# A sigmoid-attention and swish-MLP kernel on one core: its opening joins the step table, and the table is laid out anew

## The chip, the core and the metric

The kernel runs on one core of a Trainium2 chip. A core has a matrix engine (PE, or TensorE, whose weight loads the profile lists as PEld), a vector engine (DVE), a scalar engine (ACT), a general engine (POOL, or GpSimd) and a queue engine that only starts transfers here (SP). Each runs its own list of instructions in order and waits on semaphores for the others. Operands lie in SBUF, an on-chip memory of 128 partitions; PE writes its results to PSUM, eight banks of 128 x 512 float32. Transfers between main memory and SBUF (DMA) are issued by SP and POOL and carried out by 16 shared DMA engines.

The metric is the device time of one execution in microseconds (us). Three runs of the kernel before took 368.27, 368.7 and 368.22 us; their median is 368.27.

## The reference

```python
scores = q @ k.T / sqrt(64) - log(448)             # 8 batches, 12 heads, 448 tokens, 64 values a head
attn   = 1 / (1 + exp(-scores))                    # a sigmoid, no softmax
x      = (attn @ v).transpose(0, 2, 1, 3).reshape(3584, 768)
h      = x @ w_in                                  # 768 x 2048
g      = h / (1 + exp(-beta * h))                  # beta: one value for each of the 2048
out    = g @ w_out                                 # 2048 x 768
```

Everything comes and goes as float32; the kernel computes in float16 with float32 sums.

## The kernel before

The work on PE is of three kinds. *Score visits* multiply 32 rows at a time, four or more small products side by side in the array (line 221); ACT turns each PSUM tile of scores into float16 weights by a sigmoid (line 233). *Value blocks* multiply these with v in halves of 64 columns (line 294, `attend`); DVE copies the result, rounded to float16, to `xT` (line 303). *Dense steps* are the two layers of the MLP (line 174, `dense`), on the full 128 x 128 array, or cut into two halves of 64 columns where `tiled["cols"]` is 64. Most of the dense work uses Strassen-Winograd products: seven products of half-size blocks replace eight, at the price of sums of blocks on DVE.

The program is one flat order of steps, written in a table of tokens (`STEPS`) that `follow` runs one by one. A token is a letter and its numbers. `V g.jt` is a score visit for four heads (group g; three groups make a batch) and one block of keys; `A g` the value block of that group. `D b.dc` is one plain dense step of the first layer (batch b, columns dc): six matmuls, a sigmoid on ACT and a product on DVE that frees its bank. `O` is the plain second layer of the first tokens. `I b.d.i` is the i-th Winograd product of the first layer, six matmuls of 224 columns each; `I...1` is followed by an ACT copy to an output buffer, `I...2` by two ACT sigmoids, the others by DVE sums. `U t.i.part` is the same for the second layer and output tiles t and t+1: four matmuls of 384 columns each; the second part of `U...3` stores tile t, that of `U...4` tile t+1. `G` and `B` are a sigmoid on ACT and a product on POOL that reads an output buffer. `X` and `H` are token and hidden sums on DVE, `S` and `T` sums of weights on DVE (1536 elements each), `R` transposes q (`.0`) or k (`.1`) on DVE, `E` doubles a part of v. `Q g` loads q and k of a group and `K b` the v of a batch; both are issued by POOL, in POOL's order with its products. Output tiles are stored by SP, four transfers a tile.

Four buffers (`outp`, 4 x [128, 896] float32) hold both the output tiles and the intermediate results of `I`; they rotate, so a store has to land before its buffer is written again. Three buffers hold raw q and k. PSUM is shared out as two score tiles of two banks and four single banks after the opening (three score tiles and two banks before; `share_psum`). `bank` always takes the single bank that has been unused longest, so a step can wait for the copy or product that frees it. In `follow` a dense step is cut into halves if the next visit or value block is an `A`.

The opening, up to the first tokens, is no part of the table. It is written as Python: all its loads first, then transposes, six half visits (224 of 448 queries) with filler matmuls (`idle_units`, whose result nobody reads) behind each, then value blocks, further half visits and the first half (columns 0 to 223) of the plain first layer, 16 steps by `first_half`:

```python
        for n in range(2 * QPB):
            half_visit(n // 2, 0, n % 2)
            idle_units((3, 4, 4, 4, 2, 2)[n])
        double_v_last(0)
        transpose(0, 0, NH, NB)
        attend(0, 0, QH)
```

Of the kernel before, what the change touches and what calls it, by code (L numbers as in the profile page):

```python
# [13 lines left out]
def kernel(  # L14
# [267 lines left out]
    def attend(g: int, c0: int, n: int, part=(0, 1)):  # L282
# [4 lines left out]
        avs = [bank("av_ps") for _ in slots]  # L287
        order = sorted(range(JF), key=lambda jt: list(at_tiles).index((slots[-1], jt, c0)))
        todo = [(s, av, jt) for jt in order for s, av in zip(slots, avs)]
        for s, av, jt in todo + [(s, av, JF) for s, av in zip(slots, avs)]:  # L290
            at = at_tiles.pop((s, jt, c0))
            base, nk = (last_base(s), KL) if jt == JF else (0, P)
            for hh in range(2):
                nc.tensor.matmul(  # L294
                    av[hh * D : (hh + 1) * D, 0:n],
                    vs[b][base : base + nk, 2 * (s % NPAIR) + hh, jt],
                    at[base : base + nk, hh, 0:n],
                    start=(jt == order[0]),
                    stop=(jt == JF),
                    tile_position=(base, hh * D),  # L300
                )
        for s, av in zip(slots, avs):
            nc.vector.tensor_copy(out=xTs[b][:, s % NPAIR, c0 : c0 + n], in_=av[:, 0:n])  # L303
# [304 lines left out]
    todo = list(range(NDC))  # L608

    def first_half(n: int):  # L610
        for _ in range(n):
            dense1(0, todo.pop(0), 0, QH)
# [28 lines left out]
    def follow(steps):  # L641
        last_visit = max(i for i, step in enumerate(steps) if step[0] == "V")
        nearer = [""] * len(steps)
        for i in reversed(range(len(steps) - 1)):
# [9 lines left out]
        R3.1 R3.0 D0.6 D0.12 R4.1 D0.14 D0.7 V3.1 R4.0 D0.13 D0.0 D0.8 V3.0 D0.3 D0.9 V3.3 D0.1  # L654
        D0.10 E1 D0.2 Q6 V3.2 D0.4 O0.0.0 D0.5 O0.0.1 O0.0.2 V4.1 O1.0.0 O0.0.3 A3 V4.0 O1.0.1 R5.1
        D0.11 D0.15 O0.0.4 R5.0 V4.2 O0.0.5 S1.1 O0.0.6 O1.0.2 O1.0.3 S1.0 O0.0.7 S2.0 O1.0.4 V4.3
        O1.0.5 A4 V5.1 O1.0.6 O0.1.0 O0.1.1 O1.1.0 S2.1 Q7 T3.1 O1.0.7 S4.0 T2.1 O0.1.2 V5.0 T3.0
        O0.1.3 O1.1.1 K2 O1.1.2 O1.1.3 O0.1.4 O0.1.5 V5.2 T2.0 O1.1.4 O0.1.6 O0.1.7 R6.1 O1.1.5 R6.0
# [6 lines left out]
        I2.0.2 H4.1 I2.0.3 R10.1 X2.2 U4.1.0 V9.0 X2.3 U4.1.1 Q11 G2.0 U4.6.0 U4.6.1 Q12 A9 V10.0
        I2.0.7 H4.3 U4.5.0 U4.7.0 U4.5.1 V10.1 U4.7.1 I2.0.4 B2.0.1 U4.3.0 U4.4.0 U4.2.0 B2.0.0
        U4.2.1 R11.0 U4.3.1 U4.4.1 R11.1 I2.1.1 V10.2 Q13 Q14 I2.1.6 I2.1.5 I2.1.7 I2.1.2 K4 I2.1.3
        V10.3 I2.1.4 G2.1 B2.1.0 R12.1 I2.2.1 B2.1.1 A10 V11.0 I2.2.6 I2.2.5 R12.0 I2.2.7 I2.2.2
        I2.2.3 I2.3.1 Q15 G2.2 V11.1 I2.3.6 I2.2.4 B2.2.1 B2.2.0 I2.3.5 I2.3.2 R13.1 I2.3.7 I2.3.3
        V11.2 I2.3.4 B2.3.1 U6.1.0 B2.3.0 H6.2 U6.1.1 A11 H6.0 V12.2 U6.2.0 U6.7.0 H6.1 U6.2.1 G2.3  # L670
# [6 lines left out]
        B3.2.1 I3.3.2 I3.3.7 I3.3.3 V14.3 I3.3.4 U10.1.0 B3.3.0 B3.3.1 H10.2 R16.0 U10.1.1 A14 V15.2
        U10.2.0 H10.0 U10.7.0 H10.1 G3.3 U10.2.1 U10.5.0 U10.6.0 U10.6.1 H10.3 U10.5.1 X4.0 V15.0
        U10.7.1 X4.1 U10.3.0 U10.3.1 I4.0.1 I4.0.6 I4.0.5 H12.0 U10.4.0 X4.2 U10.4.1 X4.3 I4.0.2
        I4.0.3 I4.0.7 V15.1 E5 K6 G4.0 Q19 H12.2 U12.1.0 H12.1 U12.1.1 A15 R17.0 V16.1 U12.2.0 R18.1  # L680
        I4.0.4 B4.0.0 U12.6.0 B4.0.1 U12.2.1 U12.5.0 V16.2 U12.6.1 U12.5.1 I4.1.1 H12.3 I4.1.6
        U12.7.0 U12.7.1 R17.1 I4.1.5 U12.3.0 U12.3.1 I4.1.2 V16.0 R18.0 I4.1.3 U12.4.0 I4.1.7
        U12.4.1 Q20 G4.1 V16.3 I4.1.4 A16 B4.1.0 B4.1.1 R19.0 V17.2 I4.2.1 I4.3.1 I4.2.6 I4.2.5
        V17.1 I4.2.2 Q21 I4.2.7 I4.2.3 G4.2 V17.0 I4.2.4 I4.3.6 B4.2.0 I4.3.5 I4.3.7 I4.3.2 B4.2.1
        R20.0 I4.3.3 G4.3 V18.2 I4.3.4 R19.1 A17 I5.0.1 B4.3.0 X5.0 B4.3.1 U14.1.0 V18.0 I5.0.2 X5.1
        I5.0.6 Q22 I5.0.5 U14.1.1 V18.1 X5.2 X5.3 H14.0 I5.0.3 U14.2.0 E6 H14.2 K7 I5.0.7 H14.1
        V18.3 G5.0 U14.2.1 A18 V19.2 I5.0.4 U14.6.0 U14.5.0 U14.7.0 B5.0.0 U14.6.1 U14.5.1 B5.0.1
        U14.7.1 I5.1.1 V19.0 H14.3 I5.1.6 I5.1.2 U14.3.0 R21.1 U14.3.1 R20.1 V19.1 U14.4.0 E7 I5.1.5
        I5.1.7 U14.4.1 I5.1.3 V20.0 R21.0 I5.1.4 G5.1 B5.1.0 I5.2.1 B5.1.1 A19 V20.2 I5.2.6 Q23
        I5.2.5 I5.2.2 I5.2.7 I5.2.3 I5.3.1 I5.2.4 G5.2 I5.3.6 B5.2.0 V20.3 I5.3.5 I5.3.7 B5.2.1  # L690
        I5.3.2 I5.3.3 I5.3.4 V20.1 X6.0 B5.3.1 H16.2 B5.3.0 U16.1.0 U16.1.1 A20 V21.2 U16.2.0 H16.0
        U16.7.0 U16.2.1 G5.3 V21.0 H16.1 U16.5.0 R23.1 U16.6.0 U16.6.1 H16.3 U16.5.1 U16.7.1 H18.2
        I6.0.1 X6.2 V21.1 U16.3.0 X6.1 U16.3.1 U16.4.0 U16.4.1 I6.0.6 R22.1 I6.0.2 R22.0 I6.0.5 A21
        V22.0 H18.0 X6.3 I6.0.3 H18.1 U18.1.0 U18.7.0 U18.1.1 V22.1 I6.0.7 U18.6.0 U18.6.1 V22.2
        I6.0.4 H18.3 U18.5.0 G6.0 U18.2.0 R23.0 U18.5.1 U18.2.1 B6.0.1 B6.0.0 U18.7.1 V22.3 U18.3.0
        U18.3.1 U18.4.0 U18.4.1 I6.1.1 I6.1.6 A22 V23.0 I6.1.5 I6.1.7 I6.1.2 I6.1.3 I6.2.1 G6.1
        I6.1.4 B6.1.0 I6.2.6 I6.2.5 B6.1.1 I6.2.2 V23.1 I6.2.7 I6.2.3 I6.3.1 I6.2.4 I6.3.6 G6.2
        B6.2.1 I6.3.5 B6.2.0 I6.3.7 I6.3.2 I6.3.3 V23.2 I6.3.4 B6.3.1 U20.1.0 H20.2 U20.1.1 A23
        U20.7.0 B6.3.0 U22.1.0 H20.0 U20.2.0 H20.1 X7.0 U20.2.1 U20.5.0 U20.6.0 G6.3 U20.6.1 I7.0.1
        U20.5.1 H20.3 X7.2 U22.1.1 U20.7.1 I7.0.2 X7.1 U20.3.0 U20.3.1 U22.2.0 U22.2.1 H22.0 U20.4.0  # L700
        X7.3 H22.2 H22.1 U20.4.1 U22.5.0 I7.0.6 I7.0.5 U22.7.0 I7.0.7 I7.0.3 U22.6.0 G7.0 I7.0.4
        I7.1.1 I7.1.6 I7.1.5 B7.0.0 B7.0.1 I7.1.2 I7.1.7 I7.2.1 I7.1.3 I7.2.6 G7.1 I7.1.4 I7.2.5
        I7.2.7 B7.1.0 B7.1.1 U22.6.1 I7.2.2 I7.2.3 U22.5.1 H22.3 I7.2.4 I7.3.1 I7.3.6 B7.2.0 I7.3.5
        G7.2 B7.2.1 I7.3.7 U22.7.1 I7.3.2 I7.3.3 U24.1.0 I7.3.4 U22.3.0 U22.3.1 U24.1.1 U22.4.0
        B7.3.0 U22.4.1 U24.2.0 B7.3.1 H24.0 U26.1.0 U24.2.1 H24.1 U24.5.0 G7.3 U24.6.0 H24.2 U24.6.1
        U24.5.1 H24.3 H26.0 U24.7.0 U24.7.1 U26.1.1 U24.3.0 U24.3.1 H26.1 U24.4.0 U26.2.1 U26.5.0
# [159 lines left out]
```

## Time and profile before

| | |
|---|---|
| median of three runs | 368.27 us |
| span of the profiled execution | 367.6 us |
| PE, DVE, ACT, POOL busy | 361.6, 272.2, 248.7, 154.3 us |
| PE waits that the profile names, 150 ns or longer | 2.3 us in five places |
| loads issued by POOL, moved | 22.47 MB |
| stores and first loads issued by SP, moved | 11.71 MB |
| granted PE clock | 0.9 or more in each of the 40 slices |

The span goes from the first instruction of the program to the last. A group's row reads: source line, engine, operation, output and inputs by name, shapes, count, then busy time in us, mean ns of one, and the idle time of the engine before these instructions with what ended it. A row of a stretch gives its length, then the busy time of PE, PEld, DVE, ACT and POOL with the number of instructions, the granted clock, and two figures on DMA. A row of the timeline gives start, length, engine and instructions that follow each other; lengths overlap, since a matmul's end is modelled and the next one starts before it, so a step's cost is read from start to start. The chain of waits is followed back from the last instruction to whatever released it.

### The profile page before, as it was taken

Reading aid. Unit: us, or ns where it says so; the run is one execution under the profiler, and the core shown is the slowest. Engines: PE = TensorE matmul, PEld = TensorE weight load, DVE = VectorE, ACT = ScalarE, POOL = GpSimd, SP = SyncE. Lnnn points to the kernel's source line nnn. Section 1 sums busy time; section 2 is a strip of 40 time slices with the busy share of each in tenths; the row PEclk is TensorE's granted clock in tenths of the full one; section 3 lists DMA queues with packets and bytes.
Section 4 is the critical chain, followed back from the end, with each engine's and each line's share of the span. In section 5 each row is a group of like instructions: output and inputs, shape, how many; then the busy total and the mean of one; then the engine's idle time right before and its main releaser. Section 6 shows DMA issues by size and latency. Waiting matters only on the chain.

```text
span 367.6 us, 9130 instructions
## 1 busy us (share of the span) xinstructions
PE 361.6 (98%) x3677; PEld 237.7 (65%) x3677; DVE 272.2 (74%) x524; ACT 248.7 (68%) x410; POOL 154.3 (42%) x192
## 2 busy tenths in 40 slices
...
GB/s 163 182 197 201 197 206 199 237 40 2 50 139 52 165 147 2 81 57 122 143 9 153 52 137 51 50 79 88 52 1 88 2 87 2 0 87 0 61 67 134
DMA packets 42698, 34.76 MB, mean 95 GB/s; under 512 B 21904, under 2 KB 39200, under 8 KB 42656
## 3 DMA queue, kind: packets, MB, share of 16 engines
q0 software_dynamic: 36688, 22.47, 44.7%
q1 hardware_dynamic: 5968, 11.71, 11.5%
...
q14 instruction: 13, 0.11, 0.1%
...
## 4 chain that ended last, share of the span: by engine, by line
PE 94%; DMA 3%; ACT 1%; DVE 1%; SPq 0%; issue 0%; ACTq 0%; DVEq 0%
PE m_ps L174 71%; PE sco L221 12%; PE av_ps L294 10%; DMA out_dram<-osb 2%; PE idle_ps L743 1%; ACT attnT L233 1%; DMA gt<-in_k_dram 1%; DVE osb L375 0%; SPq L605 0%; ACT osb L428 0%; DVE xT L303 0%; ACT osb L466 0%; DVE raw L760 0%; SPq L726 0%; DVE kT L763 0%
## 5 line engine op out<-in xcount | busy, mean ns | idle before, releaser
L233 ACT ACTIVATE attnT<-sco 128x896 f16<-128x896 f32 (+1 forms) x163 | 139.2, 908 | 38.5 <-PE sco L221 37.9
L375 DVE TENSOR_TENSOR osb<-m_ps,osb 128x448 f32<-128x448 f32 (+2 forms) x197 | 116.3, 596 | 51.7 <-PE m_ps L174 42.2
L174 PEld LDWEIGHTS <-w_in 128*128 128x128 f16 (+1 forms) x948 | 81.0, 100 | 19.4 <-issue 11.5
L174 PE MATMUL m_ps<-xT,w_in 128*128 128x224 f16 (+3 forms) x750 | 85.5, 266 | 0.8 <-ACT osb L466 0.5
L495 POOL TENSOR_TENSOR gt<-osb,sg 128x448 f16<-128x448 f32 x26 | 29.5, 1135 | 118.4 <-ACT sg L428 108.2
L505 POOL TENSOR_TENSOR gt<-osb,sg 128x448 f16<-128x448 f32 x52 | 58.3, 1137 | 34.9 <-ACT sg L428 33.2
L428 ACT ACTIVATE sg<-osb,beta_sb 128x224 f32<-128x224 f32 (+1 forms) x104 | 54.0, 575 | 10.0 <-DVE osb L375 9.8
L174 PEld LDWEIGHTS <-sum 128*128 128x128 f16 (+1 forms) x444 | 39.9, 99 | 27.4 <-issue 3.7
L174 PEld LDWEIGHTS <-gt 128*128 128x128 f16 (+1 forms) x474 | 36.9, 102 | 25.8 <-issue 7.7
L174 PE MATMUL m_ps<-w_out,gt 128*128 128x384 f16 (+2 forms) x350 | 52.6, 324 | 0.0
L221 PE MATMUL sco<-qT,kT 32*128 32x448 f16 (+3 forms) x864 | 51.4, 340 | 0.4 <-DVE kT L763 0.2
L174 PEld LDWEIGHTS <-w_S 128*128 128x128 f16 (+1 forms) x486 | 43.9, 99 | 7.0 <-issue 6.0
L174 PE MATMUL m_ps<-w_out,sum 128*128 128x384 f16 (+1 forms) x228 | 40.6, 327 | 0.0
L174 PE MATMUL m_ps<-w_T,sum 128*128 128x384 f16 (+1 forms) x216 | 40.3, 326 | 0.0
L303 DVE CAST xT<-av_ps 128x448 f16<-128x448 f32 (+1 forms) x54 | 28.4, 566 | 14.3 <-PE av_ps L294 14.1
L294 PE MATMUL av_ps<-attnT,v 128*64 128x448 f16 (+3 forms) x400 | 38.2, 343 | 0.0
L174 PE MATMUL m_ps<-xs,w_S 128*128 128x224 f16 (+1 forms) x330 | 36.2, 259 | 0.0
L294 PEld LDWEIGHTS <-v 128*64 128x64 f16 (+1 forms) x432 | 20.5, 108 | 18.1 <-issue 10.2
L428 ACT ACTIVATE osb<-m_ps,beta_sb 128x224 f32<-128x224 f32 x52 | 20.4, 449 | 15.3 <-PE m_ps L174 13.8
L221 PEld LDWEIGHTS <-kT 32*128 32x128 f16 (+1 forms) x864 | 13.4, 96 | 23.1 <-issue 20.9
L466 ACT COPY osb<-m_ps 128x448 f32<-128x448 f32 x26 | 13.8, 536 | 18.4 <-PE m_ps L174 15.4
L135 POOL DMA_DIRECT2D v<-in_v_dram x32 | 19.9, 633 | 13.3 <-DMA w_out<-in_moe_w_out_dram 6.5
...
## 6 DMA issues: line engine op xcount, KB each, us to landing
...
w_in<-in_moe_w_in_dram POOLq DMA_DIRECT2D x8, 384.0 KB, 10.4
w_out<-in_moe_w_out_dram POOLq DMA_DIRECT2D x4, 768.0 KB, 13.1
...
```

What stands on the lines that cost most here:

```text
L135: queue.dma_start(out=to[i * BLK : (i + 1) * BLK, h0:h1, 0:JF].rearrange("p h j d -> p h (j d)"), in_=rows[:, :, JF * i * D : JF * (i + 1) ...
L174: nc.tensor.matmul(to[c : c + step], hidden[:, c : c + step], weights, **({} if step == P else {"tile_position": (0, c)}), **flags,)
L221: nc.tensor.matmul(sco[base : base + nk, hh, u0 : u0 + n], kT[g][lo : lo + BLK, jt * P : jt * P + nk, e], qT[g][lo : lo + BLK, c0 : c0 + n ...
L233: nc.scalar.activation(out=at[:, :, 0:n], in_=sco[:, :, 0:n], func=AF.Sigmoid, bias=NEG_LOG_S, scale=MSCALE,)
L294: nc.tensor.matmul(av[hh * D : (hh + 1) * D, 0:n], vs[b][base : base + nk, 2 * (s % NPAIR) + hh, jt], at[base : base + nk, hh, 0:n], start ...
L303: nc.vector.tensor_copy(out=xTs[b][:, s % NPAIR, c0 : c0 + n], in_=av[:, 0:n])
L375: nc.vector.tensor_tensor(out=out, in0=in0, in1=in1, op=op)
L428: nc.scalar.activation(out=out, in_=in_, func=AF.Sigmoid, bias=0.0, scale=beta_sb[:, dc : dc + 1])
L466: nc.scalar.copy(out=oa[:, 0], in_=m)
L495: nc.gpsimd.tensor_tensor(out=gt[:, 2 * d : 2 * d + 2, off : off + QH], in0=ob[:, 0], in1=sg, op=ALU.mult)
L505: nc.gpsimd.tensor_tensor(out=gt[:, dc, off : off + S].rearrange("p (h n) -> p h n", h=2), in0=oa[:, :, j], in1=sg, op=ALU.mult,)
L743: nc.tensor.matmul(idle[:, 0:cols], still[:, 0:P], still[:, 0:cols], start=True, stop=True)
```

## The change

The opening's steps and all its loads become tokens of one more table, `OPENING`, run by `follow` ahead of `STEPS`; the three first loads, issued by SP, the first ten filler matmuls and the first transposes stay as they are. New tokens: `h` a half visit, `y` and `z` a value block's first three products and its last one with the copy to `xT`, `f` a first-half dense step, `r` a half transpose of q, `i` filler, `l`, `k`, `v`, `w`, `o` loads of q halves, k, v, w_in and w_out, `b` the turn of beta, `p` the new sharing of PSUM. `attend` can now be run in two stages and holds its banks between them. `follow` also looks at `h`, `y` and `z` when it decides whether to cut a dense step. All of `STEPS` has a new order. Parts of the opening (six first-half dense steps `f10` to `f15`, two value blocks) move into `STEPS`.

```diff
-    def attend(g: int, c0: int, n: int, part=(0, 1)):
+    avs = {}
+
+    def attend(g: int, c0: int, n: int, part=(0, 1), stage=(0, 1)):
...
-        avs = [bank("av_ps") for _ in slots]
-        order = sorted(range(JF), key=lambda jt: list(at_tiles).index((slots[-1], jt, c0)))
-        todo = [(s, av, jt) for jt in order for s, av in zip(slots, avs)]
-        for s, av, jt in todo + [(s, av, JF) for s, av in zip(slots, avs)]:
+        if 0 in stage:
+            order = sorted(range(JF), key=lambda jt: list(at_tiles).index((slots[-1], jt, c0)))
+            for s in slots:
+                avs[s, c0] = bank("av_ps", hold=None if 1 in stage else (s, c0)), order[0]
+        todo = []
+        if 0 in stage:
+            todo += [(s, jt) for jt in order for s in slots]
+        if 1 in stage:
+            todo += [(s, JF) for s in slots]
+        for s, jt in todo:
+            av, first = avs[s, c0]
...
-        for s, av in zip(slots, avs):
+        if 1 not in stage:
+            return
+        for s in slots:
+            av, _ = avs.pop((s, c0))
+            if (s, c0) in held:
+                touch(held.pop((s, c0)))
...
+    def load_part(g: int, r: int, half: int):
+        load_one(g, r, half * NH, (half + 1) * NH)
...
+    def share_anew():
+        firsts.close()
+        share_psum(ctx, seconds, 2, N_ONE, 2)
...
+        "i": lambda n: idle_units(n),
+        "h": lambda g, half, second: half_visit(g, half * QH, second),
+        "y": lambda g, half: attend(g, half * QH, QH, (0, 1), (0,)),
+        "z": lambda g, half: attend(g, half * QH, QH, (0, 1), (1,)),
+        "f": lambda dc: dense1(0, dc, 0, QH),
...
-            nearer[i] = nxt if nxt in "VA" else nearer[i + 1]
+            nearer[i] = nxt if nxt in "VAhyz" else nearer[i + 1]
...
-            tiled["cols"] = D if then == "A" else P
+            tiled["cols"] = D if then in ("A", "y") else P
...
     STEPS = """
...
-        A5 O1.1.6 I1.3.1 V6.2 O1.1.7 S4.1 D1.8 R7.0 S3.1 D1.11 T1.1 Q8 V6.0 Q9 D1.3 R7.1 D1.2 X1.0
-        V6.1 D1.10 D1.9 E2 K3 D1.1 X1.1 V6.3 T1.0 D1.0 A6 V7.1 I1.3.6 I1.3.2 X1.2 I1.3.5 V7.0 X1.3
...
-        U8.4.1 I3.1.1 A13 V14.1 I3.1.6 K5 I3.1.5 I3.1.7 I3.1.2 I3.1.3 I3.2.1 I3.1.4 Q18 I3.2.6 G3.1
-        B3.1.0 B3.1.1 I3.2.2 I3.2.5 V14.2 I3.2.7 I3.2.3 Q17 I3.3.1 I3.2.4 G3.2 I3.3.6 I3.3.5 B3.2.0
...
+        R3.0 y1.1 z1.1 R3.1 f10 y2.1 z2.1 V3.0 f11 D0.7 D0.9 D0.0 R4.1 V3.2 D0.6 D0.1 o1.1
+        D0.3 S1.0 V3.3 D0.4 f12 D0.8 D0.12 D0.5 R4.0 S2.0 E1 V3.1 Q6 f13 D0.2 Q7 f14 D0.14
...
+        S4.0 O1.1.6 O1.1.7 A5 V6.2 R7.1 O0.1.7 T2.1 R7.0 D1.1 T4.1 D1.2 V6.1 X1.0 X1.1 D1.11
+        T1.0 D1.8 E2 D1.9 T2.0 T1.1 I1.3.1 V6.3 D1.0 A6 R8.0 S3.1 V7.1 D1.10 D1.3 X1.2
...
+        U2.6.0 X2.0 U2.6.1 H2.3 R10.0 K3 G1.2 V8.3 G1.3 U2.5.1 Q14 U2.7.1 A8 V9.1 H4.0
+        U2.3.0 U2.3.1 H4.1 U4.1.0 U4.1.1 V9.2 U2.4.0 E3 U4.2.0 U2.4.1 R11.1 X2.1 V9.0 R11.0
+        I2.0.1 U4.2.1 Q13 A9 V10.3 X2.2 S3.0 U4.6.0 U4.6.1 X2.3 I2.0.2 H4.2 I2.0.6 I2.0.5
+        H4.3 V10.0 U4.5.0 U4.5.1 Q12 K4 I2.0.3 V10.1 U4.3.0 U4.3.1 I2.0.7 G2.0 I2.1.1 R12.1
...
+        R13.0 K5 U6.2.0 X3.2 U6.2.1 I3.0.1 V12.1 U6.5.0 Q16 U6.6.0 U6.6.1 X3.1 H6.2 I3.0.2
...
+        I3.1.1 U8.3.0 I3.1.6 U8.3.1 R14.1 I3.1.2 I3.1.5 I3.1.7 U8.7.1 R15.0 I3.1.3 I3.1.4
+        V14.2 E5 Q18 U8.4.0 U8.4.1 I3.2.1 A13 G3.1 V14.0 B3.1.0 I3.2.6 I3.2.5 Q19 I3.2.7
...
+        H12.3 A16 G4.1 V17.2 Q21 I4.1.4 I4.2.1 U12.3.0 U12.3.1 B4.1.0 B4.1.1 I4.2.6 I4.2.2
...
+        U18.2.1 U18.5.1 I6.1.1 U18.7.1 U18.3.0 B6.0.0 I6.1.6 U18.4.0 U18.3.1 V22.3 U18.4.1
+        A22 V23.0 I6.1.5 I6.1.7 I6.1.2 I6.1.3 B6.0.1 I6.1.4 I6.2.1 I6.2.6 G6.1 I6.2.5 I6.2.2
...
+        U26.2.0 H26.3 U26.7.0 U26.7.1 U26.3.0 U26.3.1 U26.4.0 U26.4.1 U26.2.1
+    """.split()
+
+    OPENING = """
+        l1.0.0 k1 h0.0.0 i2 l2.0.0 k2 i2 v0 h0.0.1 l0.0.1 r1.0 R1.1 i3 l1.0.1 h1.0.0 i4 w0
+        w1 h1.0.1 w2 b0 w3 l2.0.1 R2.1 r2.0 i4 h2.0.1 w4 w5 E0 i4 h2.0.0 r0.1 y0.0 z0.0
+        h0.1.0 y1.0 z1.0 h0.1.1 Q3 y2.0 r1.1 Q4 w6 w7 z2.0 h1.1.0 p0 f0 f1 f3 f4 r2.1 h1.1.1
+        K1 f5 f2 o0.0 y0.1 Q5 z0.1 h2.1.0 f7 f6 o1.0 o0.1 f9 f8 h2.1.1
     """.split()
...
-        for g in range(1, QPB):
-            load_one(g, 0, 0, NH)
-            load_one(g, 1)
-        load_v(0)
...
-        follow(STEPS)
+        follow(OPENING + STEPS)
```

More of the change, by code (lines that the diff above doesn't have):

```diff
@@ L297, in attend @@
                     at[base : base + nk, hh, 0:n],
-                    start=(jt == order[0]),
+                    start=(jt == first),
                     stop=(jt == JF),
@@ L606, in store, with turn_beta @@
             c += n
[L608 to L612, printed above, removed]
+    def load_part(g: int, r: int, half: int):
+        load_one(g, r, half * NH, (half + 1) * NH)
+    def turn_beta():
+        for i in range(P // BLK):
+            part = slice(i * BLK, (i + 1) * BLK)
+            nc.vector.transpose(out=beta_sb[part], in_=beta_in[:, part])
+    def share_anew():
+        firsts.close()
+        share_psum(ctx, seconds, 2, N_ONE, 2)
     ALSO = {g: (g + 1,) if g > QPB and g + 1 < NQUAD else () for g in range(QPB, NQUAD)}
     RUN = {
+        "i": lambda n: idle_units(n),
[3 more added lines that the diff above has]
+        "f": lambda dc: dense1(0, dc, 0, QH),
+        "r": lambda g, half: transpose(g, 0, half * NH, (half + 1) * NH),
+        "b": lambda _: turn_beta(),
+        "p": lambda _: share_anew(),
+        "l": load_part,
+        "k": lambda g: load_one(g, 1),
+        "v": load_v,
+        "w": load_w_in,
+        "o": load_w_out,
         "V": lambda g, jt: visit(g, jt, ALSO[g] if jt == JF else ()),
@@ L653 @@
     STEPS = """
[L654 to L658, printed above, removed]
@@ L665 @@
[L665 to L670, printed above, removed]
@@ L677 @@
[L677 to L706, printed above, removed]
@@ L707 @@
-        U26.6.0 H26.2 U26.6.1 U26.5.1 H26.3 U26.7.0 U26.7.1 U24.4.1 U26.3.0 U26.3.1 U26.4.0 U26.4.1
-        U26.2.0
+        R3.0 y1.1 z1.1 R3.1 f10 y2.1 z2.1 V3.0 f11 D0.7 D0.9 D0.0 R4.1 V3.2 D0.6 D0.1 o1.1
+        D0.3 S1.0 V3.3 D0.4 f12 D0.8 D0.12 D0.5 R4.0 S2.0 E1 V3.1 Q6 f13 D0.2 Q7 f14 D0.14
+        V4.1 f15 A3 V4.0 O0.0.0 R5.1 D0.11 O1.0.0 D0.15 R5.0 S1.1 Q8 O0.0.1 V4.2 O0.0.2
+        D0.10 O1.0.1 D0.13 O1.0.2 V4.3 O1.0.3 O0.0.3 A4 V5.1 O1.0.4 O1.0.5 O0.0.4 O1.0.6 K2
+        O0.1.0 S2.1 O1.1.0 O1.1.1 O1.1.2 S4.1 V5.0 O0.0.5 O0.1.1 O0.1.2 O0.0.6 O0.1.3 T3.1
@@ new lines @@
+        U10.3.0 U10.3.1 I4.0.3 V15.0 U10.4.0 H12.2 I4.0.7 G4.0 X4.3 A15 V16.0 U10.4.1 R17.0
+        I4.0.4 H12.1 U12.1.0 I4.1.1 U12.1.1 B4.0.0 K6 I4.1.6 R18.1 B4.0.1 U12.6.0 V16.3
+        I4.1.5 I4.1.2 U12.2.0 I4.1.3 U12.6.1 U12.2.1 V16.2 U12.5.0 I4.1.7 R18.0 U12.5.1 Q20
+        H12.3 A16 G4.1 V17.2 Q21 I4.1.4 I4.2.1 U12.3.0 U12.3.1 B4.1.0 B4.1.1 I4.2.6 I4.2.2
+        I4.2.5 I4.2.7 V17.1 I4.2.3 I4.2.4 I4.3.1 G4.2 I4.3.6 V18.2 U12.7.0 I4.3.2 I4.3.5
+        B4.2.0 I4.3.7 U12.7.1 I4.3.3 B4.2.1 V17.0 U12.4.0 I4.3.4 G4.3 R19.1 U12.4.1 X5.0
@@ new lines @@
+        U14.1.0 B4.3.0 B4.3.1 U14.1.1 A17 V18.0 X5.1 H14.0 I5.0.1 K7 U14.2.0 H14.1 X5.2
+        U14.2.1 I5.0.6 E6 R21.0 R20.1 V18.3 U14.6.0 I5.0.5 H14.2 I5.0.2 U14.6.1 X5.3 Q22
+        U14.5.0 I5.0.3 V18.1 I5.0.7 H14.3 U14.5.1 A18 G5.0 V19.2 U14.3.0 U14.7.0 U14.3.1
+        U14.7.1 I5.1.1 V19.0 I5.1.6 U14.4.0 I5.0.4 B5.0.1 V19.1 I5.1.5 R20.0 I5.1.7 I5.1.2
+        R22.0 I5.1.3 G5.1 U14.4.1 I5.1.4 V20.0 R21.1 I5.2.1 I5.2.6 B5.0.0 A19 V20.2 B5.1.1
+        I5.2.5 I5.2.7 I5.2.2 I5.3.1 I5.2.3 G5.2 V20.3 I5.2.4 I5.3.6 I5.3.5 I5.3.7 Q23 B5.2.0
@@ new lines @@
+        A22 V23.0 I6.1.5 I6.1.7 I6.1.2 I6.1.3 B6.0.1 I6.1.4 I6.2.1 I6.2.6 G6.1 I6.2.5 I6.2.2
+        B6.1.0 I6.2.7 I6.2.3 B6.1.1 I6.3.1 I6.2.4 I6.3.6 I6.3.5 I6.3.7 B6.2.1 I6.3.2 I6.3.3
+        U20.1.0 B6.2.0 V23.2 H20.2 I6.3.4 X7.0 B6.3.1 B6.3.0 U20.1.1 H20.0 U22.1.0 V23.1
+        H20.1 U20.7.0 U20.2.0 G6.2 I7.0.1 U20.2.1 A23 U20.6.0 U20.6.1 X7.1 U20.5.0 U20.5.1
+        H20.3 U20.7.1 I7.0.6 G6.3 I7.0.5 H22.0 U20.3.0 U20.4.0 U20.3.1 I7.1.1 X7.3 I7.0.2
+        X7.2 I7.1.6 I7.0.7 U20.4.1 I7.1.5 U22.1.1 I7.0.3 G7.0 I7.2.1 I7.0.4 U22.2.0 H22.1
```

83 lines of the change are left out of this document (26 added, 57 removed).

## The prediction

> **What bounds the kernel now.** I read the page first, then the stretches, the chain of waits, PE's own rows and the groups by form.
>
> ```profile
> span 367.6 us, 9130 instructions
> PE 361.6 (98%) x3677; PEld 237.7 (65%) x3677; DVE 272.2 (74%) x524; ACT 248.7 (68%) x410; POOL 154.3 (42%) x192
> PE 94%; DMA 3%; ACT 1%; DVE 1%; SPq 0%; issue 0%; ACTq 0%; DVEq 0%
> ```
>
> The matrix engine (PE) is busy 98% of the span and is 94% of the chain that ended last. So a new order of steps can only win three things: idle time of PE, time that PE spends on changing between kinds of matmul, and stretched matmuls. The profiled span is 367.6 us and the median of the three runs 368.27 (368.22 to 368.7). I work on the span and add the 0.67 between the two.
>
> ```profile
> 0.00:5.42 5.42, 4.03 (x10) 1.34 (x10) 1.95 (x7) 2.09 (x4) 4.45 (x13) 1.00 0.70 171
> 5.42:19.40 13.98, 13.53 (x196) 6.17 (x197) 5.92 (x19) 12.28 (x16) 10.32 (x16) 1.00 1.39 175
> 160.00:200.00 40.00, 39.38 (x394) 27.36 (x394) 29.77 (x57) 26.19 (x45) 21.78 (x27) 1.00 0.61 93
> 364.04:367.60 3.56, 0.00 (x0) 0.00 (x0) 0.36 (x1) 0.00 (x0) 0.00 (x0) 0.87 0.55 195
> ```
>
> The second number is the length of a stretch, the third PE's busy time in it. PE idles 1.4 us at the head, 0.45 in the opening, 0.62 at 160 to 200 and 3.56 in the tail: together the 6.0 that the span has more than PE's busy time. Head and tail stay: the first loads and filler are the same, and both tables end with the same half of U26.2 behind U26.4.1. Two places are left, and the changes of kind.
>
> **The middle stall, removed: 0.95.** The chain of waits there, then PE's rows.
>
> ```profile
> 171.48 5.85 DMA out_dram<-osb
> 177.51 0.66 ACT osb L428 x2
> 178.19 1.72 ACT attnT L233 x2
> 180.37 0.64 DVE osb L375
> ```
>
> ```profile
> 177.95 0.74 PE L174 MATMUL m_ps<-xs,w_in 128*128 128x224 f16 x6
> 178.53 1.31 PE L174 MATMUL m_ps<-xs,w_S 128*128 128x224 f16 x12
> 180.38 1.31 PE L174 MATMUL m_ps<-xT,w_in 128*128 128x224 f16 x12 [0.54 <-ACT osb L466]
> 181.77 0.73 PE L174 MATMUL m_ps<-xT,w_S 128*128 128x224 f16 x6
> ```
>
> A store took 5.85 us; ACT could not write its buffer before that, the visits' sigmoids stood behind ACT's wait, and the copies and sums that free PSUM came late. Six matmuls take 0.58 from start to start, so twelve 1.15: 178.53 to 180.38 is 0.70 too long and 180.38 to 181.77 is 0.24 too long. In the new table K5 stands a pair of output tiles earlier and only Q18 stays by these stores (U8's), so I take the whole 0.95 as gone (0.4 if Q18 alone keeps half of it).
>
> **Changes of kind, removed: 0.75.** The rows that price one:
>
> ```profile
> 80.12 0.74 PE L174 MATMUL m_ps<-xT,w_in 128*128 128x224 f16 x6
> 80.70 0.74 PE L174 MATMUL m_ps<-xs,w_S 128*128 128x224 f16 x6
> 81.37 0.62 PE L221 MATMUL sco<-qT,kT 32*128 32x448 f16 x8
> 88.89 1.49 PE L174 MATMUL m_ps<-w_out,gt 128*64 128x384 f16 x16
> 90.22 1.61 PE L294 MATMUL av_ps<-attnT,v 128*64 128x448 f16 x16
> 91.76 0.57 PE L221 MATMUL sco<-qT,kT 32*128 32x448 f16 x8
> ```
>
> 80.12 to 80.70 is 0.58; the same six ahead of a score visit (80.70 to 81.37) take 0.67, so leaving wide matmuls for a visit costs 0.09. Eight pairs of half-width matmuls take 1.33, or 0.166 a pair, and run into the values with no such step; half-width is no dearer than full. In the two instruction orders, 7 of the 27 value blocks of before are followed by wide matmuls and 20 directly by a visit; after, it is 1 wide, 1 half-width and 25 visits. Two places went from wide matmuls straight into values, now none. That makes 8 fewer changes, at 0.09 about 0.75 (bounds 0.5 and 1.05). The value steps y and z ("two steps") have no PE work between them anywhere, so the split itself is worth nothing. The 88 additional matmuls are wide ones cut in two: nothing, by the pair price above.
>
> **The opening: 0.3 gained (0 to 0.6).**
>
> ```profile
> 6.04 6.28 ACT L233 ACTIVATE early<-sco 128x896 f16<-128x896 f32 x8 [0.87 <-PE sco L221]
> 12.46 3.06 ACT L233 ACTIVATE attnT<-sco 128x896 f16<-128x896 f32 x4
> 16.15 3.17 ACT L233 ACTIVATE attnT<-sco 128x896 f16<-128x896 f32 x4 [0.62 <-PE sco L221]
> 19.37 0.83 PE L174 MATMUL m_ps<-xT,w_in 128*128 128x224 f16 x7 [0.21 <-ACT attnT L233]
> ```
>
> ACT runs 16 sigmoids with one gap of 0.62: the opening is ACT's until 19.3. Filler stays at 19 matmuls, in five groups for six. The ninth half-visit now stands ahead of the first dense step, so PE gives ACT work earlier; at most ACT's 0.62 comes back, and I take half. Transposes, beta and loads are now queued among the steps: on DVE each is due well after its load, and w6 and w7 move behind Q3 and Q4 on POOL, four transfers later, while their first user, f12, now stands behind the whole opening and some 9 us of PE work (nine dense steps of 0.58, two half value blocks, three visits). No cost.
>
> **New waits: 1.3 paid.** Prices, mean ns after the comma:
>
> ```profile
> L375 DVE TENSOR_TENSOR w_T<-w_T,w_out 128x1536 f16<-128x1536 f16 x2 | 1.9, 955 | 0.0
> L323 DVE TENSOR_TENSOR gt<-m_ps,sg 128x448 f16<-128x448 f32 x8 | 4.9, 617 | 1.5 <-ACT sg L320 1.3
> L303 DVE CAST xT<-av_ps 128x448 f16<-128x448 f32 x42 | 24.2, 618 | 11.6 <-PE av_ps L294 11.5
> L466 ACT COPY osb<-m_ps 128x448 f32<-128x448 f32 x26 | 13.8, 536 | 18.4 <-PE m_ps L174 15.4 <-POOL gt L495 1.3 <-POOL gt L505 0.9
> L428 ACT ACTIVATE sg<-osb,beta_sb 128x448 f32<-128x448 f32 x52 | 32.6, 669 | 4.5 <-DVE osb L375 4.5
> L505 POOL TENSOR_TENSOR gt<-osb,sg 128x448 f16<-128x448 f32 x52 | 58.3, 1137 | 34.9 <-ACT sg L428 33.2 <-PE sco L221 1.4 <-PE m_ps L174 0.3
> ```
>
> *Weight sums bunched.* Between A5 and D1.10 DVE now has 20 instructions: five weight sums, six products of D1, three transposes, two value copies, two token sums, E2 and one output copy, the small ones near 0.5 each. That is 13.0 us, less 0.08 overlap each 11.4; PE's steps there add up to 11.5. D1.10 takes the bank that D1.0's product frees, last in this queue: 0.2 late (0 to 0.5).
>
> *A store behind loads.* U4.2.1's ACT copy writes the buffer stored after U2.3.1. PE's steps from U2.3.1 to U4.6.0, which needs the bank back, add up to 7.8; the sum on DVE (about 0.6), three issues ahead of the last store (1.4 with their gaps), the copy and hand-overs take 2.6, which leaves 5.2 for the store. On POOL, Q14 and Q13 are issued together just ahead of it.
>
> ```profile
> L605 SPq DMA_DIRECT2D out_dram<-osb x105: 314/422/1787, 63.7 to 364.5; - x105
> DMA to landing us min/median/max: 1.8/2.6/6.3
> ...
> L605 SPq DMA_DIRECT2D out_dram<-osb x8: 314/426/643, 120.7 to 124.0; - x8
> DMA to landing us min/median/max: 3.0/5.6/6.3
> ```
>
> Stores take 1.8 to 6.3; the eight issued among loads at 120.7 had a median of 5.6. So 5.6 - 5.2 = 0.4 late (0 to 1.1).
>
> *A buffer returned late.* B6.0.1 now stands between I6.1.3 and I6.1.4; I6.2.1's copy takes the buffer that it reads. From the end of I6.1.2: two half sigmoids 0.66 (the chain's second row), B6.0.1's sigmoid 0.67 less an overlap of 0.1, POOL's product 1.14, ACT's copy 0.54 and five hand-overs, about 0.3, make 3.2, while PE reaches I6.2.2 after five steps of 0.58, at 2.9: 0.3 late, and the following steps, whose sums stand behind it on DVE, again 0.4. I take 0.7 (0.3 to 1.0).
>
> **Sum.** 367.6 - 0.95 - 0.75 - 0.3 + 0.2 + 0.4 + 0.7 = 366.9; with 0.67 outside the span 367.6 us.
>
> **Rivals.** *The new waits stay away* (loads clear of the stores, DVE ahead): 367.6 + 1.3 less is 366.3. For it: PE is then a little slower than counted everywhere and gives others time. Against: the late buffer is a plain count of steps.
>
> *Stores take turns with loads.* A store then passes waiting loads, U4's 0.4 is 0, and the time 367.2. For it: the quickest of the eight took 3.0. Against: their median of 5.6 beside 1.8 for the quickest anywhere. This is a rule of the Trainium skill, DMA: Bandwidth & Descriptors, section Queues, rings and completion order: each DMA engine takes turns between the queues, packet by packet. The 5.6 does not look like it.
>
> *The opening and the changes of kind give nothing* because ACT sets that stretch (12.28 of 13.98 busy): 368.3 - 0.95 + 1.3, near 368.6. Against: only 5 of the 8 changes lie there.
>
> *Slower: stores against reused buffers.* Four output buffers rotate, and the new table spaces a store and the next writer more closely in several places, three of them a few steps behind loads: U4 behind Q12 and K4, U8 behind Q18, U12 behind Q21. If stores take 5.6 wherever a load was issued in the 5 us before, each such place costs what the middle one cost, 0.95. Three of them, with that stall's own 0.95 still counted as gone, give 367.6 + 2.85 - 0.4, about 370.0; from two on the run is slower than before. For it: SP's issue has a maximum of 1787 ns beside a median of 422, which delays stores at random. Against: the loads are mostly placed away from them.
>
> **How the numbers follow.** Forecast 0.42 (366.9 to 368.3), waits stay away 0.16, stores take turns 0.08, nothing from opening and kinds 0.15, stores against buffers 0.19. A run of this kernel can be told from no change from about 0.2%, here 0.74 us: 367.53 to 369.01. The forecast lies on the lower edge, so half of its chance counts as faster, with the two cases below it: faster 0.44, same 0.37, slower 0.19. The range 366.2 to 369.5 takes the first four cases whole and the milder part of the last.
>
> **What would show it.** Right: no PE gap near 175 to 182; no store on the chain; the PE rows ahead of visits with fewer 0.09 steps; short waits of PE at D1.10, U4.6.0 and I6.2.2. Wrong: ACT or DVE waiting on output stores in more than two places, or PE idle in the opening above 0.45.

## The result, and the profile after

| kernel | median (lowest to highest) | ratio to before, 95% interval | span of the profiled execution |
|---|---|---|---|
| before | 368.49 us (368.22 to 369.32) | | 367.6 us |
| changed | 372.76 us (372.0 to 375.03) | 1.012 (1.0094 to 1.0146) | 370.9 us |

The change makes the kernel slower by 1.2%. The forecast was 367.6 us, a little faster, and the predicted range ended at 369.5. The page of the changed kernel and then its waits of PE, which give the engine and line waited for, total, number of times and the longest:

```profile
span 370.9 us, 9301 instructions
PE 361.5 (97%) x3765; PEld 238.9 (64%) x3765; DVE 278.9 (75%) x524; ACT 247.9 (67%) x410; POOL 156.4 (42%) x192
```

```profile
PE m_ps L174 <- ACT osb L597: 1.7, 1, 1.7
PE m_ps L174 <- DVE sum L389: 1.6, 2, 1.0
...
PE m_ps L174 <- ACT osb L480: 0.4, 1, 0.4
PE m_ps L174 <- DMA w_in<-in_moe_w_in_dram: 0.3, 1, 0.3
PE m_ps L174 <- DVE gt L337: 0.3, 1, 0.3
PE m_ps L174 <- DVE osb L389: 0.2, 1, 0.2
```

PE is as busy as before. What is new is waiting. DVE's busy time has grown by 6.7 us although it runs the same 524 instructions. Read from start to start, as in the prediction, the new gaps of PE are these, each with the start of the last matmul ahead of it (the waits above are a little shorter than the gaps, since a matmul's modelled end hides their beginning):

| at, us | step that comes late | predicted | found | waits for |
|---|---|---|---|---|
| 20.8 | f4 | 0 | 0.50 | a load of w_in |
| 76.1 | D1.10 | 0.2 | 0.35 | D1.0's product on DVE |
| 93.9 | H2.0's and H2.1's users | 0 | 0.23 | DVE's sums |
| 109.3 | U4.6.0 | 0.4 | 1.75 | U4.2.1's ACT copy, that for a store |
| 238.9 | I step | 0 | 0.20 | not followed |
| 272.4 | U16.6.0 | 0 | 1.09 | DVE's sum H16.1 |
| 303.9 to 309.9 | I6.2 and I6.3 | 0.7 | 1.19 | the buffer that B6.0.1 reads |
| 318.4 | user of H20.1 | 0 | 0.66 | DVE's sum H20.1 |

They make 5.97. On the other side 0.95 is gone with the middle stall, and PE's own steps, at the median distance of each kind, add up to 1.05 less. The remaining 0.7 between this and the span's +3.3 is smaller gaps in the opening (0.4) and a shorter tail (0.3).

The step U4.6.0, first. PE and ACT of the changed kernel:

```profile
109.01 0.60 PE L221 MATMUL sco<-qT,kT 32*64 32x448 f16 x16
...
110.76 0.48 ACT L597 COPY osb<-m_ps 128x384 f32<-128x384 f32 x1 [2.23 <-DMA out_dram<-osb]
...
111.29 0.97 PE L174 MATMUL m_ps<-w_T,sum 128*128 128x384 f16 x5 [1.68 <-ACT osb L597]
```

The place is the predicted one. The transfers issued from 100 to 108 us, with their median from issue to landing at the end, show why the size was wrong:

```profile
out_dram<-osb SPq DMA_DIRECT2D x8, 96.0 KB, 5.4
raw<-in_q_dram POOLq DMA_DIRECT2D x2, 224.0 KB, 5.7
raw<-in_k_dram POOLq DMA_DIRECT2D x2, 224.0 KB, 7.1
```

The first four of the eight stores, those that the copy needs, landed 5.9 to 6.7 us after their issue, the last of them at 110.66. The slowest load, issued just ahead of them at 102.46, took 8.96.

The gap at 272 shows what the prediction had not counted at all:

```profile
271.34 0.68 DVE L389 TENSOR_TENSOR sum<-gt 128x1024 f16<-128x1024 f16 x1
...
272.01 1.14 POOL L509 TENSOR_TENSOR gt<-osb,sg 128x448 f16<-128x448 f32 x1 [1.50 <-ACT sg L442]
272.06 1.64 DVE L389 TENSOR_TENSOR sum<-sum,gt 128x1024 f16<-128x1024 f16 x1
...
273.75 1.47 PE L174 MATMUL m_ps<-w_T,sum 128*128 128x384 f16 x8 [1.02 <-DVE sum L389]
```

H16.0 takes 0.68 us. H16.1, the same size, starts 0.05 after POOL's product G5.3 and takes 1.64: it ends at 273.70, 0.55 after the product's end at 273.15. So nearly all of its work came after POOL was done. Two later profiles in which this place is left as it is (those of the moved B6.0.1 and of the moved loads, below) show the same gap of 1.09. The line of DVE's sums, kept apart by inputs (minimum, median, maximum in ns), first before, then after:

```profile
L375 DVE TENSOR_TENSOR osb<-m_ps,osb x197: 358/624/626, 80.3 to 364.1; 128x448 f32<-128x448 f32 x130, 128x384 f32<-128x384 f32 x65, 128x192 f32<-128x192 f32 x2
...
L375 DVE TENSOR_TENSOR sum<-gt x26: 649/685/799, 89.8 to 356.6; 128x1024 f16<-128x1024 f16 x26
...
L375 DVE TENSOR_TENSOR sum<-sum,gt x13: 681/685/693, 94.3 to 355.4; 128x1024 f16<-128x1024 f16 x13
L375 DVE TENSOR_TENSOR sum<-gt,sum x13: 651/682/684, 98.8 to 359.3; 128x1024 f16<-128x1024 f16 x13
```

```profile
L389 DVE TENSOR_TENSOR osb<-m_ps,osb x197: 358/616/626, 80.8 to 367.6; 128x448 f32<-128x448 f32 x130, 128x384 f32<-128x384 f32 x65, 128x192 f32<-128x192 f32 x2
...
L389 DVE TENSOR_TENSOR sum<-gt x26: 650/682/1297, 89.7 to 359.7; 128x1024 f16<-128x1024 f16 x26
...
L389 DVE TENSOR_TENSOR sum<-sum,gt x13: 670/684/1641, 94.4 to 357.8; 128x1024 f16<-128x1024 f16 x13
L389 DVE TENSOR_TENSOR sum<-gt,sum x13: 653/681/1449, 97.1 to 363.4; 128x1024 f16<-128x1024 f16 x13
```

The medians agree; the maxima of the sums of two SBUF inputs do not. Both traces hold 80 sums of token and hidden blocks. In the new order 15 of them start while a product runs on POOL, in the old order 1. All 16 end at a fixed distance behind that product's end: 0.55 to 0.59 us with 1024 elements, 0.36 to 0.37 with 672. The 15 take 7.6 us more than they would at 0.68 and 0.50 each, which covers DVE's 6.7. The one of the old order, at 184.3, is the maximum of 799 in its `sum<-gt` row: the old trace did hold a price for the meeting, in a maximum and not in a mean. One sum of the new order, at 97.1, took 1.45 with no product running when it started; POOL was issuing loads then, and this was not followed.

Sums with one input in PSUM (the first row of each) do not show it: their longest is 626 ns in both kernels. The Trainium skill states this rule in SBUF — State Buffer, section Who interferes with whom: "A DVE instruction with two SBUF inputs contends with a GpSimd instruction that reads SBUF", and whichever issues first blocks the other for its whole length. The rows agree in the first point, and in the second up to 0.13 us: the later one ends 0.55 after the other, where it takes 0.68 alone.

### The profile page after: what moved, and what is told of

It is laid out like the page before. It is cut to its first block, busy times and chain, and to the rows that moved or that the text cites. A ratio compares the mean times of both kernels' runs of the same rounds, so it can differ in the third digit from the quotient of the medians.

```text
span 370.9 us, 9301 instructions
## 1 busy us (share of the span) xinstructions
PE 361.5 (97%) x3765; PEld 238.9 (64%) x3765; DVE 278.9 (75%) x524; ACT 247.9 (67%) x410; POOL 156.4 (42%) x192
## 5 line engine op out<-in xcount | busy, mean ns | idle before, releaser
L519 POOL TENSOR_TENSOR gt<-osb,sg 128x448 f16<-128x448 f32 x52 | 60.1, 1170 | 76.4 <-ACT sg L442 76.2
L509 POOL TENSOR_TENSOR gt<-osb,sg 128x448 f16<-128x448 f32 x26 | 30.0, 1153 | 77.9 <-ACT sg L442 73.8
L442 ACT ACTIVATE sg<-osb,beta_sb 128x448 f32<-128x448 f32 (+1 forms) x104 | 55.0, 577 | 6.1 <-DVE osb L389 6.0
```

Source lines behind the costliest of these rows:

```text
L442: nc.scalar.activation(out=out, in_=in_, func=AF.Sigmoid, bias=0.0, scale=beta_sb[:, dc : dc + 1])
L509: nc.gpsimd.tensor_tensor(out=gt[:, 2 * d : 2 * d + 2, off : off + QH], in0=ob[:, 0], in1=sg, op=ALU.mult)
L519: nc.gpsimd.tensor_tensor(out=gt[:, dc, off : off + S].rearrange("p (h n) -> p h n", h=2), in0=oa[:, :, j], in1=sg, op=ALU.mult,)
```

## The experiments

Below, the mended kernel is the one under *All of it together*. Spans are given against 370.9 (changed) or 367.6 (before). In every run here 1.7 to 2.2 us lie between the span and the time of the same execution.

**One product moved.**

```diff
-... H16.1 U16.2.0 E7 G5.3 U16.2.1 I6.0.6 V21.1 U16.6.0 U16.6.1 X6.3 ...
+... H16.1 U16.2.0 E7 U16.2.1 I6.0.6 V21.1 U16.6.0 U16.6.1 G5.3 X6.3 ...
```

> The changed kernel with one token moved: G5.3 stands behind U16.6.1, three halves of U steps later, no more right behind H16.1. Theory A (product against sum): a sum on DVE whose two inputs lie in SBUF stands still while POOL multiplies out of SBUF; H16.1 took 1.64 us in the changed kernel with G5.3's product beside it, 0.68 is the rule. It should be back at 0.68, PE's gap of 1.09 at 272 should be gone, and the span should be about 1.1 us shorter than the changed kernel's 370.9. Theory B (DVE is simply late there, its queue too full): the sum stays late, the gap keeps 0.7 or more, the span changes by less than 0.3.

The stretch of this kernel:

```profile
271.79 0.69 DVE L389 TENSOR_TENSOR sum<-sum,gt 128x1024 f16<-128x1024 f16 x1
271.89 0.57 PE L221 MATMUL sco<-qT,kT 32*128 32x448 f16 x8
...
272.53 1.47 PE L174 MATMUL m_ps<-w_T,sum 128*128 128x384 f16 x8
```

H16.1 takes 0.69, PE's gap falls from 1.09 to 0.14, and the span is 369.7, 1.2 less. This is theory A. The median, 372.7 us, ratio 1.0099 (1.0076 to 1.0123), does not show it: it is that of the changed kernel within a spread of 2.5 us between runs.

**The same token moved the other way, in the kernel before.**

```diff
-... U16.2.1 G5.3 V21.0 H16.1 U16.5.0 ...
+... U16.2.1 V21.0 H16.1 G5.3 U16.5.0 ...
```

> The kernel before with one token moved as the change has it: G5.3 right behind H16.1 (it stood two steps ahead of it). Theory A (product against sum): H16.1 becomes longer, from 0.68 to between 1.0 and 1.6, if the product starts first, or the product becomes longer, from 1.14 to about 1.5, if the sum does; PE gets a gap of 0.3 to 1.0 near 275, and the span grows by as much from 367.6. Theory B (no contention, only queue order): no sum becomes longer, the span stays within 0.2.

```profile
269.57 0.69 DVE L375 TENSOR_TENSOR sum<-sum,gt 128x1024 f16<-128x1024 f16 x1
...
272.62 0.68 DVE L375 TENSOR_TENSOR sum<-gt,sum 128x1024 f16<-128x1024 f16 x1
272.69 1.61 POOL L495 TENSOR_TENSOR gt<-osb,sg 128x448 f16<-128x448 f32 x1 [3.89 <-ACT sg L428]
```

The product did not reach H16.1, the first row, which had ended at 270.26. The move made it start 0.8 later than in the kernel before, and it met the next sum, H16.3. That was luck, but it shows the other order of the two: the sum starts 0.07 earlier, and the product takes 1.61 instead of 1.14, ending 1.00 after the sum's end. Nobody was waiting for it, PE has no gap, and the time is unchanged: 368.68 us, ratio 0.9991 (0.9981 to 1.0002). The growth of 0.3 or more that theory A expected did not come. A product that starts ahead of the sum was not produced in the kernel before by this move.

**A product moved ahead of its buffer's next user.**

```diff
-... U18.3.0 B6.0.0 I6.1.6 ... I6.1.3 B6.0.1 I6.1.4 ...
+... U18.3.0 B6.0.0 B6.0.1 I6.1.6 ... I6.1.3 I6.1.4 ...
```

> The changed kernel with one token moved: B6.0.1 stands right behind B6.0.0, ahead of I6.1.6. Theory A (buffer returned late): the three PE gaps at 304 to 310 (0.60, 0.24 and 0.35, together 1.19) go, the span falls by 1.2. Theory B (the ACT queue sets this stretch, whichever the order): the gaps move and the span falls by less than 0.4. The gap of 0.66 at 318 stays or grows in both, since POOL's products there are not moved.

The changed kernel, then this one, at the same steps:

```profile
302.82 1.31 PE L174 MATMUL m_ps<-xs,w_S 128*128 128x224 f16 x12
304.57 1.31 PE L174 MATMUL m_ps<-xT,w_in 128*128 128x224 f16 x12 [0.43 <-ACT osb L480]
305.95 0.74 PE L174 MATMUL m_ps<-xT,w_S 128*128 128x224 f16 x6
```

```profile
302.98 1.31 PE L174 MATMUL m_ps<-xs,w_S 128*128 128x224 f16 x12
304.13 1.31 PE L174 MATMUL m_ps<-xT,w_in 128*128 128x224 f16 x12
305.28 0.74 PE L174 MATMUL m_ps<-xT,w_S 128*128 128x224 f16 x6
```

Twelve matmuls take 1.15 again instead of 1.75 and 1.38; of 1.19 in three gaps 0.17 is left. That is theory A at this place. The span (370.1) fell by only 0.8: the gap at 318 grew from 0.66 to 0.75, and at 93, where DVE's sums stand behind a transpose that waits for a load, the first step was 0.91 late in this execution instead of 0.17, while f4's gap shrank by 0.3. The median is 372.2 us, ratio 1.0095 (1.0069 to 1.012).

**Old and new order spliced.** The old stretch stands between U2.6.1 and I2.2.3 and behind U12.4.1; at the joints K3, G1.3, E3 and E4 are set so that each load is there in time, and R20.0 is moved.

> The new table up to U2.6.1 and from I2.2.3 to U12.4.1, the old order in between and behind. By the times at which PE reaches the same place in both kernels the new order gains 0.36 up to U2.6.1, loses 1.74 from there to I2.2.3 (nearly all of it at U4.6.0, where a store is waited for), gains 0.94 from there to U12.4.1 (the middle stall), and loses 3.15 behind. Theory A (the loss is local, at a few places): this kernel has the two gains alone, 1.3 less than the kernel before, a span near 366.3, 0.35% faster. Theory B (what one stretch gains comes back as waits in the next, because engines off the path and transfers set the pace): 367.3 or more.

The profiled execution had a span of 366.0, as theory A has it, but the median is 368.96 us, ratio 0.9997 (0.9982 to 1.0011), and the spans of its runs go from 365.9 to 368.3. New gaps of 0.24 and 0.39 arose at 131.7 and 147.6, on both sides of the second joint. Neither theory is settled by it. It only shows that the largest losses are absent where the new order is left out.

**The loads moved off the store.**

```diff
-... U2.5.1 Q14 U2.7.1 ... U4.2.1 Q13 A9 ... Q12 K4 I2.0.3 ...
+... U2.5.1 n14 U2.7.1 ... U4.2.1 n13 A9 ... Q12 K4 m14 m13 I2.0.3 ...
+        "n": lambda g: [load_one(g, r, 0, 1) for r in (0, 1)],
+        "m": lambda g: [load_one(g, r, 1, NB) for r in (0, 1)],
```

> The changed kernel, where Q14 and Q13 stand now only load the first of 14 column blocks (four transfers of 1/14 of the size), and the rest of them is loaded behind K4; buffers and every other step stay. Theory A (the store waits behind loads): the four stores behind U2.3.1 land within 4 us instead of 5.9 to 6.7, U4.2.1's copy no longer waits for them, PE's gap of 1.75 at 109 goes, the span falls by 1.6 to 1.8 from 370.9. Theory B (the copy is late for another reason, DVE's sum or the issue by SP): the gap keeps 1.0 or more. The gaps at 272, 304 to 310 and 318 stay.

Transfers issued from 100 to 108 us, then ACT and PE, in this kernel:

```profile
out_dram<-osb SPq DMA_DIRECT2D x8, 96.0 KB, 2.1
raw<-in_q_dram POOLq DMA_DIRECT2D x2, 16.0 KB, 2.4
raw<-in_k_dram POOLq DMA_DIRECT2D x2, 16.0 KB, 2.3
```

```profile
108.68 0.51 ACT L597 COPY osb<-m_ps 128x384 f32<-128x384 f32 x1
...
109.28 0.60 PE L221 MATMUL sco<-qT,kT 32*64 32x448 f16 x16
...
109.82 1.47 PE L174 MATMUL m_ps<-w_T,sum 128*128 128x384 f16 x8
```

With the bytes of the loads elsewhere the same eight stores land in 2.1 us instead of 5.4, the first four of them in 1.8 to 2.5, and the gap of 1.75 is gone. This is theory A. Span 369.3, 371.25 us, ratio 1.0066 (1.0042 to 1.0089).

**Three products moved at the end.** The two moves above and a third:

```diff
-... I6.2.4 I6.3.6 I6.3.5 ... H20.1 U20.7.0 U20.2.0 G6.2 I7.0.1 ...
+... I6.2.4 I6.3.6 G6.2 I6.3.5 ... H20.1 U20.7.0 U20.2.0 I7.0.1 ...
```

> The changed kernel with three tokens moved behind 260 us: G5.3 behind U16.6.1, B6.0.1 behind B6.0.0 (both tried alone before), and G6.2 from behind U20.2.0 to behind I6.3.6, so that its product runs 4 us or more ahead of H20.1. Theory A (product against sum): H20.1 goes from 1.53 to 0.68, and the gap of 0.66 at 318 goes with those of 1.09 at 272 and 1.19 at 304 to 310: span 2.7 to 3.0 shorter than 370.9. Theory B (H20.0 waits for B6.3's products anyway, so that H20.1 is late with or without G6.2): the gap at 318 keeps 0.5 or more, the span falls by 2.0 to 2.4. The gap of 1.75 at 109 stays in both.

```profile
315.04 0.69 DVE L389 TENSOR_TENSOR sum<-gt 128x1024 f16<-128x1024 f16 x1 [2.06 <-POOL gt L519]
...
315.28 1.61 PE L303 MATMUL av_ps<-attnT,v 128*64 128x448 f16 x16
...
315.77 0.69 DVE L389 TENSOR_TENSOR sum<-sum,gt 128x1024 f16<-128x1024 f16 x1
...
316.83 1.47 PE L174 MATMUL m_ps<-w_T,sum 128*128 128x384 f16 x8
```

H20.0 still waits 2.06 for POOL, as theory B says, but that wait is covered by the value block: H20.1 takes 0.69 instead of 1.53 and PE's gap is gone, as theory A has it. Span 368.3, 2.6 less, between what the two theories gave; 370.68 us, ratio 1.0059 (1.0039 to 1.0079).

**All of it together,** with R9.1 behind H2.1 and T1.1 behind A6:

```diff
-... T2.0 T1.1 I1.3.1 V6.3 D1.0 A6 R8.0 ... V8.1 R9.1 U2.7.0 H2.0 H2.1 Q11 ...
+... T2.0 I1.3.1 V6.3 D1.0 A6 T1.1 R8.0 ... V8.1 U2.7.0 H2.0 H2.1 R9.1 Q11 ...
```

> The changed kernel with the two edits above together (loads split, three tokens moved) and two more: R9.1 behind H2.1, so that H2.0 does not stand behind a transpose that waits for a load, and T1.1 behind A6, so that D1.0's product comes 0.95 earlier for D1.10. Theory A (the gaps are local and independent of each other): 370.9 less 1.75, 1.09, 1.19, 0.66, 0.2 and 0.3, so a span near 365.7; with the 1.8 that lies outside the span in the runs so far about 367.5 us, against 368.5 to 369.0 of the kernel before: 0.3 to 0.4% faster. Theory B (mended gaps come back as others, as the product in the splice's stretches did): span 366.8 or more, no faster than before.

The span is 366.0 and the median 368.12 us, ratio 0.9977 (0.9966 to 0.9988): a little faster than the kernel before, by 0.23% where 0.3 to 0.4 was expected. In these runs 2.1 to 2.2 us lie outside the span and not 1.8. The gaps were local and their removal added up, to 4.9 of the expected 5.2. What is left is 0.51 at 24 (a half visit that waits for a load of q), 0.12 at f4 and three of 0.13 to 0.16. Still, 15 sums start under a product and DVE is busy for 277.0 us, 4.8 more than before the change: the meetings are nearly all still there, and cost time only where PE waits for the sum.

**The opening's loads.**

```diff
-        ... w2 b0 w3 l2.0.1 R2.1 ... f0 f1 f3 f4 r2.1 h1.1.1 K1 f5 f2 ...
+        ... w2 b0 l2.0.1 w3 R2.1 ... f0 f1 f3 f2 r2.1 h1.1.1 K1 f5 f4 ...
```

> The mended kernel with two changes in the opening: f2 ahead of f4, so that the third chunk of w_in is asked for two steps later, and the second half of q of group 2 loaded ahead of the fourth chunk of w_in. Theory A (in the opening PE waits for loads, in f4 or in the ninth half visit, 0.5 us in one of the two): both gaps go, 0.5 shorter than the mended kernel's span of 366.0, and 0.3% or more faster than the kernel before. Theory B (ACT's sigmoids set the opening, the load wait hides another): the same span within 0.2.

Its waits of PE:

```profile
PE idle_ps L786 <- DVE gt L779: 1.2, 1, 1.2
PE sco L221 <- DVE kT L806: 0.2, 1, 0.2
```

The load waits are gone and nothing replaces them at their place, but the profiled span is 366.0 again, as theory B has it. Against the mended kernel's execution PE was 0.39 late behind the first half visit, ahead of anything that was edited. From there to the visit at 24.6 it gained 0.64, as theory A has it, and 0.19 of that was lost again by 30.7, which was not followed. The median is 367.83 us, ratio 0.9969 (0.9955 to 0.9984). That is the lowest made here, 0.29 below the kernel without these two edits, but the intervals of the two ratios overlap, so a gain in time is not shown.

**No half-width steps.**

```diff
-            tiled["cols"] = D if then in ("A", "y") else P
```

> The mended kernel (all edits so far) without the cut of dense steps into halves: no step is half-width any more, so each of the 27 value blocks behind dense steps of the table, and those of the opening, is entered from full-width matmuls. Theory A (a change of kind costs 0.09): some 27 to 30 more changes, 2.3 to 2.8 us longer. Theory B (a change of kind costs nothing and the gain of 0.75 had another source): within 0.3 of the mended kernel.

```profile
281.22 0.81 PE L174 MATMUL m_ps<-w_out,gt 128*128 128x384 f16 x4
281.87 0.74 PE L174 MATMUL m_ps<-xs,w_in 128*128 128x224 f16 x6
282.54 1.64 PE L303 MATMUL av_ps<-attnT,v 128*64 128x448 f16 x16
```

Six wide matmuls ahead of a value block take 0.67 from start to start, 0.09 more than among themselves. The instruction order has 197 changes between wide, value and score matmuls against 173 of the mended kernel (181 before the change), and the median is 370.4 us, 2.28 more: 0.095 for each of the 24. (The kernel before, measured beside each of the two, took 368.89 and 368.81.) This is theory A, with 24 changes for the 27 to 30 that I had counted. The Trainium skill, TensorEngine Tiling (Array Packing), section Key Properties, says that a change of tiling mode drains the engine. A change from wide to value matmuls costs 0.09 here by the rows and 0.095 by the time.

**The kernel before once more.**

> The kernel before, unchanged, for a second profile. Theory A (the middle stall of 0.95 belongs to the one execution that was profiled, whose span of 367.6 lies above most others): PE's gaps of 0.70 and 0.24 near 180 are absent or smaller when the span is below 367.0, and the stores there land within 5 us. Theory B (the stall is the kernel's): it is there in every execution. Outside the span lie 1.7 to 1.9 us by the other kernels' runs, not the 0.67 of the prediction.

```profile
178.52 1.31 PE L174 MATMUL m_ps<-xs,w_S 128*128 128x224 f16 x12
179.93 1.31 PE L174 MATMUL m_ps<-xT,w_in 128*128 128x224 f16 x12
181.32 0.73 PE L174 MATMUL m_ps<-xT,w_S 128*128 128x224 f16 x6
```

Twelve matmuls should take 1.15: the two gaps are 0.26 and 0.24, half of the first profile's 0.95, in an execution with a span of 366.9. In the kernel before with G5.3 moved they were absent (span 366.4). The size follows the stores: the last one landed at 177.33 in the first profile, at 176.88 in this one, 0.45 earlier, as the gaps are 0.45 smaller, and at 175.88 where there was none. The stall belongs to the kernel, but its size differs between executions; why the stores land at different times was not followed. The ratio is 0.9993 (0.998 to 1.0006).

## Why the prediction was wrong

*The base, 367.6 and 0.67.* The prediction took the profiled execution for a run of 368.27. In later runs of this kernel about 1.9 us lie outside the span (1.85 to 2.03), and executions with a span of 367.6 took about 369.5. So the profiled execution was one of the longer ones of this kernel, with a larger middle stall than in the two later profiles. The forecast span of 366.9 would have been about 368.8 us, by its own sum. This is also why the medians differ by 4.3 us and the profiled spans by only 3.3.

*Middle stall, 0.95 removed.* It is gone in the new order, as said. But 0.95 was one execution's; two further ones had 0.50 and none. A typical execution had less to win.

*Changes of kind, 0.75 removed.* Right: eight fewer, at 0.095 each by the kernel without half-width steps, make 0.76. *New waits at D1.10* (0.35 for 0.2) and the *late buffer* (1.19 for 0.7, above its bounds of 0.3 to 1.0) are right in place and mechanism, and undersized.

*The opening, 0.3 gained.* The ninth half visit does run ahead of the dense steps, and these start no later:

```profile
18.58 0.65 PE L221 MATMUL sco<-qT,kT 32*128 32x224 f16 x16
19.16 1.90 PE L174 MATMUL m_ps<-xT,w_in 128*128 128x224 f16 x18
21.39 0.75 PE L174 MATMUL m_ps<-xT,w_in 128*128 128x224 f16 x6 [0.34 <-DMA w_in<-in_moe_w_in_dram]
```

But the "no cost" of the loads failed: it looked at f12, the first user of w6 and w7, and not at f4, which stands fourth now and asks for the third chunk of w_in before it has landed. The 0.58 of the half visit that now runs ahead is given back by a gap of 0.50.

*The store behind loads, 0.4 with bounds 0 to 1.1.* Here a term of the sum failed in size. The place and the chain were right; the latency of 5.6 was a median of one group of stores, and the upper bound came from a maximum of 6.3. The needed stores took 5.9 to 6.7; the last took 6.6 where 5.2 were allowed, which makes 1.4 of the 1.75, and the rest was not followed. The rival in which a store passes waiting loads was wrong in its price: the four stores did land ahead of the last load issued before them (111.42), and still took 5.9 to 6.7, against 1.8 to 2.5 with those loads' bytes elsewhere.

*What was not in the sum at all: 1.75.* H16.1 and H20.1 cost 1.09 and 0.66. The prediction priced every DVE sum at its mean of before and moved POOL's products freely; no term and no rival named a sum beside a product. The means of before were all but unstretched, since its order kept the two apart; only the one maximum of 799 ns spoke against it. The slower rival, with 370.0 by stores at three places, foretold the sign and not the cause: of its three places only U4 became a PE gap, and behind Q14 and Q13, not behind the loads that the rival named.

So the failed steps are, by size: sums beside products (1.75 not counted), the store at U4 (1.35 above its term), the load of w_in (0.50 instead of nothing), the late buffer (0.5), and the base (about 1.2). The first two alone turn the forecast gain of 0.7 into a loss.
